# A gated linear-attention block and an MLP on one core: v's scratch copied in whole runs, two level masks in one multiply, and a new written-out order

## The chip, the core and the metric

The kernel runs on one core of a Trainium2 chip. The core has five engines that each run their own instruction stream in order and meet through semaphores: TensorE (PE, matrix products), VectorE (DVE, elementwise work on two operands), ScalarE (ACT, elementwise functions and copies), GpSimd (POOL) and SyncE (SP, which here issues every DMA). The metric is the device time of one execution in microseconds (us), taken as the median of repeated runs.

## What is computed

Inputs are float32: `q, k, v, a_re, a_im` of shape (4 batches, 8 heads, 768 tokens, 48), and an MLP with `w_in` (384 x 2048), `w_out` (2048 x 384) and `alpha` (2048).

```python
mag = np.sqrt(a_re * a_re + a_im * a_im)
scale = np.minimum(mag, 0.999) / (mag + 1e-06)
a_re_n, a_im_n = (a_re * scale, a_im * scale)
for t in range(S):
    ar, ai = (a_re_n[:, :, t, :, None], a_im_n[:, :, t, :, None])
    new_re = ar * S_re - ai * S_im
    new_im = ar * S_im + ai * S_re
    kv = np.einsum('bhd,bhe->bhde', k[:, :, t], v[:, :, t])
    S_re, S_im = (new_re + kv, new_im)
    y[:, :, t] = np.einsum('bhd,bhde->bhe', q[:, :, t], S_re)
x = y.transpose(0, 2, 1, 3).reshape(B * S, H * D)
h = x @ w_in
g = np.maximum(h, 0.0) + alpha * np.minimum(h, 0.0)
return g @ w_out
```

## The kernel before, in words

**Tiling.** The 768 tokens of a batch are cut into six chunks of 128, so there are 24 *units* u0 to u23 (batch 0 is u0 to u5, batch 1 is u6 to u11, and so on). A unit is one chunk of all eight heads. Units of a batch follow each other, because the state `St` goes from one to the next.

**Gates.** `gates` turns `a_re, a_im` into decays and rotations. It is called nine times: for batch 0 in pieces of one, two and three chunks, for each later batch in two pieces of three chunks. It writes decays to a DRAM scratch (`decs`, line 323) and rotations to another (`phs`, lines 421 and 431). The last VectorE instruction of a gate piece is the second L429; then `phs` is stored, and the first unit of that piece loads it as `PP` (L587) before it can begin with its L661. u0, u1, u3, u6, u9, u12, u15, u18 and u21 are the units that stand first behind a gate piece.

**A unit.** It loads `KQ` (keys and queries, L579 and L581), `PP` (L587), `T` (decays, L594), `V` (L603 to L608) and `VL` (L626 and L629). VectorE rotates keys and queries (L661, L663). Then three *visits* handle two levels each: (1, 2), (4, 8) and (16, 32). At level h the queries in the second half of each block of 2h tokens meet the keys of its first half: copies into `WQ` or `W` on ScalarE (L740, L756), 16 small matmuls per level into `ps_lv` (L678), and a decay step of all keys and queries on VectorE (L717, six per unit). What does not belong to the block is cleared by a mask: levels 1, 2, 4, 8 by a VectorE multiply that reads `ps_lv` and writes the tile `A` (L702, one per level), levels 16 and 32 by ScalarE copies with per-row scales (L699). Then transposes of the keys (L785, with copies L787 and L788), the state update (L797, L826, L829), and the output `ps_y` from the masked scores (L808 opens it, L817 multiplies `A` by `VL` over the six levels) and from the state (L841). ScalarE copies `ps_y` into the unit's `T` tile (L855), which is stored to the DRAM scratch `ysc` (L860).

**VL and its scratch.** `VL` holds, for each level, the rows of v that are keys there. Levels 1, 2 and 32 are loaded from v (ten DMAs, L626). Levels 4, 8 and 16 (`SPREAD`) come from a DRAM scratch `vsc`, which `half_rows` fills from v: for each batch, level and pair of heads one DMA (L560) picks the rows of all six chunks, in pieces of 96 floats. For chunk 0 of batch 0 there is a smaller scratch of its own, filled first by 12 DMAs. A unit reads its part of the scratch with one DMA into 128 partitions (L629).

**MLP.** Units are grouped: m0 is u0, m1 is u1, m2 is u2 and u3, and so on in pairs up to m11, then m12 is u22 and m13 is u23. Once the units of a group have stored `ysc`, it is loaded as `xT` (L873). For each of 16 blocks of 128 features, `features` does three matmuls (L889), a ScalarE step (L896) and a VectorE step (L898), and `outputs` multiplies by `w_out` into `ps_o` (L908). `ps_h` has two buffers, so TensorE can be two blocks ahead of L898. The weights arrive as 64-bit words and are rebuilt as float32 by ScalarE, GpSimd and VectorE (L507 to L519) during the first 180 us.

**The order.** All this is written as generators (tasks). Each `yield` marks a step. `ORDER` is one string in which a letter stands for a task (A to I the gate pieces, J the loads of units, K `half_rows`, L `loads_v`, M the raw weights, N and O the two weights' rebuilding, P to Z and a to m the units, n the loads of `xT`, o the MLP). `plan.run(ORDER)` advances the named task by one step per letter, and so sets the order of instructions on every engine and of the DMAs on SP's queue. The arguments of `DVE(...)`, `ACT(...)`, `DMA(...)`, and the rings `R[...]`, were inputs for making the string; when the kernel is built they do nothing. Semaphore waits are put in afterwards from the tiles that instructions share.

Of the kernel before, what the change touches and what calls it, by code (L numbers as in the profile page):

```python
# [18 lines left out]
P = 128  # L19
# [11 lines left out]
    "AAAAAAAAAMJBMMMMMAAAAAAAAAOAAAAAKAAAABAAAAAAAAAKAAKAKKKKKKKKKAAOAKBOKOBOBJAANBNAABBBNAAAOAAAAAANNAMA"  # L31
    "AAAAKNANABNNAAAANBAAAAABJBBBANABMBMABAOAONJOABAAABBBBBMBAAAABAAOBAABAABBBBKOBBBBBBBBBNNNNNBBJNBBPBBN"
    "BOBBBJJOJOOONBBBBPPBPBLBBLLOBPCCBBBBBLLKLLNNNJPPPCBBBBBBLPBBBBBPBPBBLLLLMPOCBMCBBPPPBBMBBCCCCLBKBBLN"
    "KNKOBKBBCBCPCCCBBCCCCCCOOCOPCCKCCJOCCPCPDDCCJJCPPCOPCPPCDNNNNDMJPJPPCPPPPPPPPPPPPPCNCQCPJOOCQOCMDDDD"
    "DCLOPCPLPPLLCQLKQJLCQLCMCQJDKLLLJQQJCQNQPCPPPPPQQQCDDCQQCNONCNKQCQQMCOOLOOCOQQJCDDDDQCnOKOOJOCRLOOCo"
    "ooQLQQCCCRDLQQQQKQQDKCDMoCNDCQKQQQDDQQQQCRCOCoLRooRooCLOLCDDLCLLDLCLLoLCDDDDCRRCoLJoJJQoCCRooCCLoKLJ"
    "ooooCoooCLRRooCooCRCQCRQQQQQQCDRQQRoooooRRCCRCCCoooCoRRoCCRQRCRNNNNRRCRRRRRRRRRRRRRNMNCNNRNNCDRDoooo"
    "oRooJDNNooooDRooRORDRoOOooODOSooooJJooEoSoRRRoooSoDooooOooEoSSSSSSoooooJNLLLLJLLLELSDSoEDEEooooSooSR"
    "SSSooDEoooSSnSDooooooooRooJDJJSSSSSSSSSSSSJTLSLDEooLLDDDDLLDJTDSDDDDDDSSSSJSToSSSEoooooooSoTooTSSSDS"
    "JJSTJJEESSKTooLooooLoTTTLLooooooJTJoooUTTLTToToToToDTDDoDoDDKDoDKLLLLLLooooLoLoLnUEEoUoDooUooTTTTToo"  # L40
    "DEoDUTDooUooUoTTTTTooJoooEooooTTEoEEooooTTTTUTTUUUUooDTDEDDoDDoDDDDLDLDoDoooDLoKUUKToLELELoTTTUUoooE"
    "LoLooLLDLUDooooLDoUDEEDEEEoEoEooooUooDDDDoDooUUKUUUooooooLJTUUUUoooUDTTTTUToooJDJooDDDDoDoooUUooEUUU"
    "UUUFoEooEUooEoooEooooJoEJEFoEEoEoooUUooEEEoUooUUUUUoEooEoEEVooooooooooooEoVVFEoVJooJJJJJooooFFJnoVFo"
    "oooJoVVVoJJVJLoooLLLVLooLLVVVLooLoFLEEEEEEEVEEEEEEEELEEEWEWEEJoEooEooooVVVFFVooooWooooVVooVWoooooooo"
    "VEWVEVoVoWWVVVFFVVFoEooWoooVLVoooLLFVooVVVVWWWVVVVJLLLWWWLLEEEWooLWWWWoLEoLLLoXoLoEEEEFEooooooVVWWWW"
    "WWVVWVoVXoWWVVoVoVoooooFLooLLJoJJFJEEFEEEWEEEoooEoEEoooWoWoKooooWWWWWWWWooWKWFWWXWWXoooWooFXXXXLoooX"
    "XXXooFFLLLLLLLLLWLWELELoooooooooFoFXEXooFooJWEoXFoXXonooooooFFLFJJJFXFoXoFooJJJoJJXXoXFXGooooooooXXo"
    "FFFooFXXXXXooFoFFooXFoooFooYXXXXXXXXXXXXXXXXXXoooFoYYYGFJJooFLoooYYYFFFFFFYYooooLLYooGooYooooZJJJYKJ"
    "GZooYGJYYYYooFLFFFFFLFLLLFLooooFZoYYoooooooZZZZZYYYYoYYLYLLZZoooGJZLLYoYooFYoFYFoooFYYoFZGKoFoFFFKFo"
    "oZZZYKKKZYYYYYYYGLGZZoFFKKZKoKFFFFFFFoFFFLLLLLoLLFoFoooZZoZZYYYYLooZooooFGoooLYFFGYYYZYoFFFFFFoooGLL"  # L50
    "ooooooLaLZZZnoFJoZoJoooJFFFFFZZFZooooooooGoooooGZGZZZZZZZZZZZZZLZZaoaoGZoGooLGoooooooooooaaaaaJoJoLJ"
    "ooJJGoGoaJaabbJJJoobooooLoooLaoaaaaaooGoooooaabbLLLLLLGLGoooooHHoooooaaaaaaLoGoGGGGGaaaoGGoGaooaooob"
    "oGHoGaaobGbbabobbaaaaaoooaooLLLLbooGoGbbHHbGaGaGaaGoaoaoaaoobbbbLooGoGGGGJGJJGGGoGJJGoGJGoGJoGHooooo"
    "oboooooooooHHHLLLLcccnooooHocoobbbbbbbccbHcoooJbooJHoooLLocLbbLoLoGoooocbcobcKooooooHHdHbbbbKbGLbGGG"
    "GbGGbGGLGGGGLbbbLGbbbbbbLLoGoHHHHoHooLLLLoooKccccccooocoHLooooocoooccocHLGGGdoGGoooHJJHGHGHGGHGLdcoc"
    "coccHcccHLHooooHoooocoddddccccccdoHLLcHcLLLLLLGGLLoLooooLLdGdLGGdGGGoGooKoooddcdccccccccHcGdGdoodooo"
    "oHoooooooooGGGGooooooooHoooodoooonKooodoooodddddddGooooHJooJHHoddddoJJJJJJJoooJIoodooeddddddddHddedd"
    "ddddddeooooooooJeJJJLJJJoooooeoeeooeooooooHeeHeHeHHHHHHHoooooooooooLooeLeeeLLLHeoLHfHHoHHLofoooooooo"
    "oooeoLeofLoJooLoLooeLfeLffeeeeeoeoeHoHoHHKHHHHHHHHHHJeooeeoofefeeeeeffHIHIHeHeHeHeeeeeeeeeoJogfoofJL"
    "LoLoooLfLffffLoLooLooLLffLooKoKKoooooooHHHHHoofffogHoHIHHfoLoLfHLIofoKgIoooooHoogggggHoofffffgogHHoH"  # L60
    "HnHogHoooooooffoofffffofgggJfLLLLLoooogggggofofoooogHHgJLLIIfoffLLLoooHooHfgffLooJffooIoLHooLoIggoII"
    "oIooooggoooooIIIIooooogooogoogoogogIIIgooogggggggIggoJIJJJhgJhgogoogKIIhhhhoJoIooogIohIIhhhgILLLhhoo"
    "ohJLJJJJLLLLLoooLLLoooooooLoKoooioohiohhhoohhooihhooooIoooohhhIiIIiiohoooooiIioIhiIoooooLhhhhhhJJIJJ"
    "ooiiooonhhoooooohhhhhohLhhhhhhLLLhhIhIihhoLJLoJJJJLIIIIIIIIIIIIIIIIIooiiiiioooooooojIoooooooooiooooL"
    "LiooojojLjLooIIIIIIIILIIIIIIILoooojijioioioojjLiiiiiojooiioooooooIoIioIIoiojjjoooooiiiiiiiiiiiIIIIII"
    "LILiiiLLooLLLLoooLIIIIIIIIILoojjLooojjiiiLLoooooooIojjoLIIjoooooooIooIIJJJonooojjjjjjjjJjJooooooJooo"
    "oooojooojjooooojjjjjjjLjjjjjjjjjjjkokooooookoooooookkkkooLoooooookookokokooLLLLJLLookJooLLLLoookkooo"
    "ooJJJJJJkokkkooooookoooookkkkkkkkkooooookokooooookoLoLkkkkkkkLLlkJkkkkkkkkkkLLooloooLLLooLoLoJoooJoo"
    "ooooooooollllolloooolloJoJoolloooooooooolllllmloooLnooooLooooooLoooLllllooollllmloooooooolooollooooo"
    "ooooolloooooLmomllllllllllllllllLloLLLLLLoooLmmLmLmoooLoooommoomoooooooomoonoooooooooLoooooooooommmm"  # L70
    "mooLoooooooooooooommoooommmoommoomoomooooooooooommmmoooooooommoooooooommmmmmmmmmmmmmoooooooooooooooo"
    "oooooomoooooooooooooooooooooooooooooooooooooooooooonoooooooooooooooooooooooooooooooooooooooooooooooo"
    "oooooooooooooooooooooooooooooooooooooooooooooooooooooooooooooooooooooooooooooooooooooooooooo")
# [28 lines left out]
def kernel(  # L102
# [64 lines left out]
    masks, by_row = {}, {}  # L167
# [3 lines left out]
    def mask(h):  # L171

        m = work.tile([P, P // h, h], F32, tag="WQ0", name="mask", bufs=1)
        nc.gpsimd.memset(m, 1.0)
        nc.gpsimd.affine_select(out=m, in_=m, pattern=[[-h, P // h], [0, h]], base=0,
                                channel_multiplier=1, compare_op=ALU.is_ge, fill=0.0)
        nc.gpsimd.affine_select(out=m, in_=m, pattern=[[h, P // h], [0, h]], base=h - 1,
                                channel_multiplier=-1, compare_op=ALU.is_ge, fill=0.0)
        masks[h] = consts.tile([P, HC], F32, tag=f"mask{h}", name=f"mask{h}")
        flat = m.rearrange("p n h -> p (n h)")  # L180
        for i in range(2):
            nc.gpsimd.tensor_copy(masks[h][64 * i:64 * i + 64],
                                  flat[64 * i:64 * i + 64, HC * i:HC * (i + 1)])
# [22 lines left out]
    for name in LEVELS:  # L206
        R[name] = Ring(2 if name <= 4 else 1)
# [286 lines left out]
    def to_f32(dst, *key):  # L494
# [25 lines left out]
        slots.append(slot)  # L520
        return t
# [19 lines left out]
    def half_rows():  # L541


        for b, chunks in [(0, 1)] + [(b, NCH) for b in range(B)]:
            vsc = dram.tile([len(SPREAD), chunks, 2, HC, 2 * D2], F32, tag=f"vsc{chunks}", name="vsc")
            for c in range(1 if (b, chunks) == (0, NCH) else 0, chunks):
                vsc_of[b * NCH + c] = vsc[:, c]
            for i, h in enumerate(SPREAD):
                for n in range(HP):
                    src = v[b, n].rearrange("(m s h) c e -> s m h c e", s=2, h=h)[0]  # L550
                    src = bass.AP(tensor=src.tensor, offset=src.offset + NCH * D2, ap=src.ap)
                    dst = vsc[i, :, n // 2, :, (n % 2) * D2:(n % 2 + 1) * D2].rearrange(
                        "c (m h) e -> m h c e", m=src.shape[0])
                    if chunks == 1:
                        dst, src = dst[:, :, 0], src[:, :, 0]

                    k = (HP * i + n) * NCH // (HP * len(SPREAD))
                    end = yield DMA(24.5 * chunks, ("KQ", (b - 1) * NCH + k) if b else
                                    ("raw", "in", k // 3 if chunks == 1 else k))
                    nc.sync.dma_start(dst, src)  # L560
            for c in range(1 if (b, chunks) == (0, NCH) else 0, chunks):
# [35 lines left out]
    def loads_v():  # L597
        for u in range(NU):
# [13 lines left out]
            for k, h in enumerate(LEVELS):  # L612
                for i in range(2):
# [8 lines left out]
                    for dst, src in runs:  # L622
                        if not first:
# [3 lines left out]
            t = yield DMA(98 * len(SPREAD), ("halves", u))  # L627
            k = LEVELS.index(SPREAD[0])
            nc.sync.dma_start(VL[:, k:k + len(SPREAD)].rearrange("p l n e -> p l (n e)"),  # L629
                              vsc_of.pop(u).rearrange("l i t e -> (i t) l e"))  # L630
# [14 lines left out]
    def unit(u):  # L645
# [37 lines left out]
        def mask_out(name, t, e):  # L683

            n = HC

            if name in by_row:
                e = yield ACT(HP * name + 100, e, takes=(R[name],))
            else:
# [311 lines left out]
```

## Time and profile before

| what | value |
|---|---|
| median of 3 runs | 852.85 us (852.84 to 853.85) |
| span of the profiled execution | 853.8 us |
| PE busy | 702.5 us (82%), 11,488 records |
| DVE busy | 650.8 us (76%), 1,020 instructions |
| ACT busy | 441.3 us (52%), 937 instructions |
| POOL busy | 203.3 us (24%) |
| DMA | 130.91 MB, 153 GB/s on average |
| DMA packets | 194,174, of them 74,120 under 512 B |

"Busy" is the time in which at least one instruction of the engine was running. A float32 matmul leaves two records, one per pass, so 1,344 records of L889 are 672 matmuls. The span is the profiled execution's own time; it lies 0.1% above the median of the runs. In the profile the letter after an engine's name, as in SPq, stands for its instruction queue.

### The profile page before, as it was taken

Reading aid. Unit: us, or ns where it says so; the run is one execution under the profiler, and the core shown is the slowest. Engines: PE = TensorE matmul, PEld = TensorE weight load, DVE = VectorE, ACT = ScalarE, POOL = GpSimd, SP = SyncE. Lnnn points to the kernel's source line nnn. Section 1 sums busy time; section 2 is a strip of 40 time slices with the busy share of each in tenths; the row PEclk is TensorE's granted clock in tenths of the full one; section 3 lists DMA queues with packets and bytes.
Section 4 is the critical chain, followed back from the end, with each engine's and each line's share of the span. In section 5 each row is a group of like instructions: output and inputs, shape, how many; then the busy total and the mean of one; then the engine's idle time right before and its main releaser. Section 6 shows DMA issues by size and latency. Waiting matters only on the chain.

```text
span 853.8 us, 26837 instructions
## 1 busy us (share of the span) xinstructions
PE 702.5 (82%) x11488; PEld 534.1 (63%) x11488; DVE 650.8 (76%) x1020; ACT 441.3 (52%) x937; POOL 203.3 (24%) x293
## 2 busy tenths in 40 slices
PE   0000428678999898999999799999999999999998
PEld 0000416557777676776677577777777777777776
DVE  5999989998998799778999686788896754643212
ACT  7848786565736444564567333456544333332211
POOL 6322142306526202440036400530006100000000
PEclk9999858689999999899999899999999999999999
DMA  6796784875398369747874479357654455421000
GB/s 202 235 245 211 219 226 137 246 188 142 98 275 182 77 159 242 187 112 182 222 202 105 129 195 206 96 144 192 151 174 100 135 132 133 108 51 35 20 28 10
DMA packets 194174, 130.91 MB, mean 153 GB/s; under 512 B 74120, under 2 KB 185864, under 8 KB 194056
## 3 DMA queue, kind: packets, MB, share of 16 engines
q1 hardware_dynamic: 194056, 129.20, 57.8%
q8 instruction: 90, 1.47, 0.7%
q14 instruction: 28, 0.23, 0.1%
HBM read 100.82 MB, written 35.71 MB: 160 GB/s over the span
## 4 chain that ended last, share of the span: by engine, by line
PE 62%; DVE 17%; DMA 11%; issue 4%; ACT 3%; SPq 2%; DVEq 0%; ACTq 0%
PE ps_o L908 24%; PE ps_h L889 23%; DVE KQ L717 4%; PE ps_lv L678 4%; PE ps_y L817 4%; DMA T<-decs 4%; PE ps_kv L797 3%; PE ps_y L841 2%; DVE gate L426 2%; PE ps_kt L785 2%; DMA PP<-phs 2%; DMA gate<-in_a_re_dram 1%; DVE gate L298 1%; DMA phs<-gate 1%; DVE gate L318 1%
## 5 line engine op out<-in xcount | busy, mean ns | idle before, releaser
L889 PE MATMUL ps_h<-xT,w_in_sb 128*128 128x256 f32 (+1 forms) x1344 | 305.3, 358 | 10.7 <-DMA xT<-ysc 8.2
L908 PE MATMUL ps_o<-w_out_sb,g_sb 128*128 128x384 f32 x768 | 293.8, 498 | 5.2 <-DVE g_sb L898 4.2
L889 PEld LDWEIGHTS ps_h<-xT,w_in_sb 128*128 128x128 f32 x1344 | 234.6, 194 | 82.9 <-DMA xT<-ysc 8.4
L898 DVE SCALAR_TENSOR_TENSOR g_sb<-g_sb,al,ps_h 128x256 f32<-128x256 f32 (+1 forms) x224 | 97.2, 436 | 116.9 <-ACT g_sb L896 116.5
L896 ACT ACTIVATE g_sb<-ps_h 128x256 f32<-128x256 f32 (+1 forms) x224 | 78.7, 352 | 204.3 <-PE ps_h L889 203.1
L717 DVE TENSOR_TENSOR KQ<-KQ,T 96x1024 f32<-96x1024 f32 x120 | 148.1, 1234 | 40.3 <-PE ps_lv L678 34.5
L908 PEld LDWEIGHTS ps_o<-w_out_sb,g_sb 128*128 128x128 f32 x768 | 139.4, 193 | 58.7 <-DVE g_sb L898 7.9
L678 PE MATMUL ps_lv<-WQ 96*32 96x32 f32 x2304 | 34.0, 202 | 78.7 <-DVE WQ L661 50.6
L678 PEld LDWEIGHTS ps_lv<-WQ 96*32 96x32 f32 x2304 | 26.1, 115 | 99.2 <-DVE WQ L661 50.6
L740 ACT COPY WQ<-KQ 96x1024 f32<-96x1024 f32 x48 | 50.0, 1042 | 27.0 <-DVE KQ L717 26.8
L515 POOL TENSOR_SCALAR top<-top 128x768 f32<-128x768 f32 x16 | 45.8, 2862 | 73.5 <-ACT top L507 62.8
L855 ACT COPY T<-ps_y 48x256 f32<-48x256 f32 x96 | 30.9, 364 | 51.6 <-PE ps_y L841 50.9
L817 PE MATMUL ps_y<-A,VL 64*48 64x64 f32 x2304 | 45.4, 232 | 14.4 <-issue 13.4
L338 POOL TENSOR_TENSOR gate<-gate 128x72 f32<-128x72 f32 x42 | 27.5, 654 | 118.1 <-ACT gate L368 115.3
L817 PEld LDWEIGHTS ps_y<-A,VL 64*48 64x48 f32 x2304 | 43.1, 133 | 15.4 <-issue 14.2
L338 DVE TENSOR_TENSOR gate<-gate 128x576 f32<-128x576 f32 (+5 forms) x84 | 47.9, 571 | 1.3
L699 ACT ACTIVATE A<-ps_lv,columns 128x64 f32<-128x64 f32 x144 | 36.9, 335 | 20.4 <-PE ps_lv L678 20.4
L756 ACT COPY W<-KQ 96x512 f32<-96x512 f32 x48 | 30.7, 639 | 30.0 <-DVE KQ L717 24.9
L426 DVE TENSOR_TENSOR gate<-gate 128x1152 f32<-128x1152 f32 (+2 forms) x36 | 43.4, 1231 | 2.1 <-POOL gate L411 2.0
L678 PE MATMUL ps_lv<-KQ,W 96*32 96x32 f32 x1536 | 24.3, 204 | 17.8 <-ACT W L756 15.8
L702 DVE TENSOR_TENSOR A<-ps_lv,mask 128x256 f32<-128x256 f32 x96 | 37.4, 411 | 0.0
L787 ACT COPY T<-ps_kt 128x384 f32<-128x384 f32 x48 | 23.1, 480 | 26.8 <-PE ps_kt L785 26.7
(106 smaller groups left out, 904.8 us busy)
## 6 DMA issues: line engine op xcount, KB each, us to landing
T<-decs SPq DMA_DIRECT2D x48, 384.0 KB
PP<-phs SPq DMA_DIRECT2D x24, 387.0 KB
KQ<-in_q_dram SPq DMA_DIRECT2D x48, 192.0 KB
decs<-gate SPq DMA_DIRECT2D x7, 1152.0 KB
phs<-gate SPq DMA_DIRECT2D x14, 576.0 KB
KQ<-in_k_dram SPq DMA_DIRECT2D x40, 192.0 KB
vsc<-in_v_dram SPq DMA_DIRECT2D x48, 144.0 KB
VL<-vsc SPq DMA_DIRECT2D x24, 288.0 KB
```

Of the source, the lines that this page charges most:

```text
L338: on(4 * k).tensor_tensor(out=m, in0=w[:, 1::-1].unsqueeze(2).to_broadcast([P, 2, 2, k]), in1=pairs_of(u), op=ALU.mult)
L426: TT(out=m[:, a], in0=U5[:, 1 + a], in1=turned(off3, o)[:, a].unsqueeze(1).unsqueeze(3).to_broadcast([P, L // 2, nb, 2]), op=ALU.mult)
L515: nc.gpsimd.tensor_scalar(out=top, in0=top, scalar1=F64_SMALL, scalar2=None, op0=ALU.max)
L678: nc.tensor.matmul(t[64 * i + j:64 * i + j + HC // 2, p], lhsT=keys(n, g), rhs=queries(n, g), start=True, stop=True)
L702: nc.vector.tensor_tensor(out=a.rearrange("p n (g t) -> p n g t", g=2), in0=t.unsqueeze(2).to_broadcast(whole), in1=masks[name].rearrange( ...
L717: nc.vector.tensor_tensor(out=x, in0=x if x0 is None else x0, in1=m, op=ALU.mult)
L740: nc.scalar.copy(z.rearrange("p i n t -> p i (n t)").rearrange("p i (m h) -> p m i h", h=h), bass.AP(tensor=KQ.tensor, offset=KQ.offset + ...
L817: nc.tensor.matmul(o, lhsT=Vp[h][64 * i:64 * i + 64, s, e_ * D:(e_ + 1) * D], rhs=a, start=False, stop=False)
L889: nc.tensor.matmul(p, lhsT=w_in_sb[:, f // 2, kk, f % 2 * P:(f % 2 + 1) * P], rhs=x_of[m][:, kk], start=(kk == 0), stop=(kk == NK - 1))
L896: nc.scalar.activation(gt, p, AF.Relu, scale=-1.0)
L898: nc.vector.scalar_tensor_tensor(out=gt, in0=gt, scalar=al_1[:, f:f + 1], in1=p, op0=ALU.mult, op1=ALU.add)
L908: nc.tensor.matmul(sums[0], lhsT=gt[:, c * P:(c + 1) * P], rhs=w_out_sb[:, f], start=(f == 0), stop=(f == NF - 1))
```

## The change

Three things are changed, and `ORDER` is replaced.

1. `half_rows` copies per batch, level and *two* pairs of heads one run of rows: source and destination have h whole rows of v (all six chunks, h x 2,304 bytes in one piece). There are 24 such DMAs, 288 KB each, where there were 60 (48 of 144 KB and 12 of 24 KB). The scratch has a new layout with the pair of heads outermost and the chunk inside, and the separate scratch for the first chunk is gone. A unit now reads the scratch in two DMAs, one for each half of the partitions, in pieces of 96 floats where they were 192.
2. The two masks of a visit lie in one tile, and one VectorE multiply clears both levels. Levels 1 and 2 share an `A` tile with two buffers, levels 4 and 8 one with a single buffer (level 4 had two, level 8 one).
3. `ORDER` is a new string of 4,232 letters; the old one had 4,292. Nearly every letter stands elsewhere. The rings' counts follow.

```diff
 ORDER = (
-    "AAAAAAAAAMJBMMMMMAAAAAAAAAOAAAAAKAAAABAAAAAAAAAKAAKAKKKKKKKKKAAOAKBOKOBOBJAANBNAABBBNAAAOAAAAAANNAMA"
...
+    "AAAAAAAAAAAAAJJMABBBAAAAAMMMMJJMLABBAAAAAAAABAABAAAANBBAAAAAAABABBNBNOBNABNANAABBBOANOOBABBBBBMABABAO"
...
-        masks[h] = consts.tile([P, HC], F32, tag=f"mask{h}", name=f"mask{h}")
+        at, first = VISIT[h]
+        if h == first:
+            pairs[first] = consts.tile([P, 2, HC], F32, tag=f"mask{h}", name=f"mask{h}")
+        masks[h] = pairs[first][:, at]
...
-        for b, chunks in [(0, 1)] + [(b, NCH) for b in range(B)]:
-            vsc = dram.tile([len(SPREAD), chunks, 2, HC, 2 * D2], F32, tag=f"vsc{chunks}", name="vsc")
-            for c in range(1 if (b, chunks) == (0, NCH) else 0, chunks):
-                vsc_of[b * NCH + c] = vsc[:, c]
+        one = NCH * D2
+        for b in range(B):
+            vsc = dram.tile([HP // 2, len(SPREAD), 2, HC, NCH, D2], F32, tag="vsc", name="vsc")
+            for c in range(NCH):
+                vsc_of[b * NCH + c] = vsc[:, :, :, :, c]
             for i, h in enumerate(SPREAD):
-                for n in range(HP):
-                    src = v[b, n].rearrange("(m s h) c e -> s m h c e", s=2, h=h)[0]
...
-                    nc.sync.dma_start(dst, src)
+                for s in range(HP // 2):
+                    rows = v[b, 2 * s]
+                    src = bass.AP(tensor=rows.tensor, offset=rows.offset + one, ap=[[2 * h * one, P // h], [1, h * one]])
+                    end = yield DMA(150)
+                    nc.sync.dma_start(vsc[s, i].rearrange("n (m h) c e -> (n m) (h c e)", h=h), src)
...
-            t = yield DMA(98 * len(SPREAD), ("halves", u))
             k = LEVELS.index(SPREAD[0])
-            nc.sync.dma_start(VL[:, k:k + len(SPREAD)].rearrange("p l n e -> p l (n e)"),
-                              vsc_of.pop(u).rearrange("l i t e -> (i t) l e"))
+            for i in range(2):
+                t = yield DMA(49 * len(SPREAD), ("halves", u))
+                nc.sync.dma_start(VL[HC * i:HC * (i + 1), k:k + len(SPREAD)].rearrange("p l n e -> p (l n) e"),
+                                  vsc_of[u][i].rearrange("l n t e -> t (l n) e"))
...
+        def mask_both(visit, t, e):
+
+            first = visit[0]
+            e = yield DVE(2 * HP * HC, e, takes=(R[first],))
+            a = work.tile([P, 2, HP, HC], F32, tag=f"A{first}", name=f"A{first}", bufs=2 if first == 1 else 1)
+            whole = [P, 2, HP, 2, HC // 2]
+            nc.vector.tensor_tensor(out=a.rearrange("p l n (g t) -> p l n g t", g=2), in0=t.unsqueeze(3).to_broadcast(whole),
+                                    in1=pairs[first].rearrange("p l (g t) -> p l g t", g=2).unsqueeze(2).to_broadcast(whole),
+                                    op=ALU.mult)
+            for at, h in enumerate(visit):
+                A[h] = a[:, at]
             made.append(e)
             return e
...
-            for h, ta, e in tiles:
-                e = yield from mask_out(h, ta, e)
+            if visit[0] in pairs:
+                e = yield from mask_both(visit, shared[0], e)
+            else:
+                for h, ta, e in tiles:
+                    e = yield from mask_out(h, ta, e)
```

Line numbers in the changed kernel are four or five higher than before from the middle on; the text keeps the numbers of the kernel before.

## The prediction

> **What bounds the kernel now.** I read the engine totals first, then the 40 slices, then the windows of 50 us, and at last the waits of single lines.
>
> ```profile
> span 853.8 us, 26837 instructions
> PE   0000428678999898999999799999999999999998
> DVE  5999989998998799778999686788896754643212
> PEclk9999858689999999899999899999999999999999
> ...
> PE 62%; DVE 17%; DMA 11%; issue 4%; ACT 3%; SPq 2%; DVEq 0%; ACTq 0%
> ```
>
> TensorE does nothing for four slices, fills up by the ninth and stays full to the end; VectorE is full from the second slice to about the twelfth. Two stages, then: first VectorE sets the pace, later TensorE does. The windows (length, then busy time and count of PE, PEld, DVE, ACT, POOL, then granted clock, DMA share, GB/s) put numbers on it.
>
> ```profile
> 50.00:100.00 50.00, 9.73 (x346) 8.22 (x346) 49.00 (x87) 39.60 (x55) 13.42 (x8) 1.00 0.81 232
> 100.00:150.00 50.00, 25.71 (x656) 21.55 (x656) 45.68 (x89) 37.20 (x64) 15.34 (x8) 0.66 0.65 180
> 150.00:200.00 50.00, 38.40 (x798) 30.71 (x799) 46.58 (x67) 28.73 (x61) 13.71 (x18) 0.80 0.74 205
> 200.00:250.00 50.00, 47.73 (x865) 37.41 (x865) 47.51 (x72) 28.89 (x72) 21.96 (x29) 1.00 0.59 165
> 250.00:300.00 50.00, 44.68 (x720) 33.51 (x719) 38.76 (x53) 29.36 (x63) 21.20 (x34) 0.97 0.65 142
> 500.00:550.00 50.00, 50.00 (x870) 38.02 (x869) 37.96 (x55) 20.15 (x51) 13.31 (x32) 1.00 0.75 184
> ```
>
> Of 151.3 us without PE work (853.8 - 702.5), 90.3 lie before 100 us, 24.3 and 11.6 in the next two windows.
>
> I turn this into one figure per unit. TensorE's work has the same instructions in both kernels. At full clock the chain shows 1.29 us for six records of L889 at 256 columns (0.43 per matmul; I take 0.22 at 128) and for four of L908 (0.645 per matmul), some 1.3 for 96 of L678, 1.4 for 96 of L817, 1.9 for 64 of L797, 0.94 for 32 of L841. Over the whole program that makes 692.2 us. The moment when a unit opens its output (its first L808) plus the PE work that still stands behind it in the order is a floor for the end. In the trace of before this floor rises so: u0 96.9 + 686.6 = 783.5; u1 132.9 + 677.6 = 810.5; u2 823.1; u3 832.4; u4 836.1; u5 836.1; u6 837.7; u7 842.0; u8 840.9; u12 847.0; u14 853.5, and about 850 from there on. Most is lost by u4, under VectorE's pace; a new order can earn by putting more PE work in front of these moments, or by letting VectorE reach them sooner.
>
> **Part 1, the double mask.** The rows:
>
> ```profile
> L702 DVE TENSOR_TENSOR A<-ps_lv,mask 128x256 f32<-128x256 f32 x96 | 37.4, 411 | 0.0
> L829 DVE TENSOR_TENSOR St<-St,ps_kv 96x384 f32<-96x384 f32 x44 | 24.1, 547 | 11.1 <-PE ps_kv L797 8.6
> L898 DVE SCALAR_TENSOR_TENSOR g_sb<-g_sb,al,ps_h 128x256 f32<-128x256 f32 x160 | 75.4, 474 | 69.0 <-ACT g_sb L896 68.7
> L661 DVE TENSOR_TENSOR WQ<-KQ,PP 96x1024 f32<-96x1024 f32 x24 | 29.4, 1227 | 4.9 <-DMA PP<-phs 4.9
> ```
>
> No row has 512 elements out of PSUM. 256 cost 411 ns and 384 cost 547, 1.06 ns per element, which leads to 683 at 512. Bounds: half of L661's 1,227, or 614, with no fixed cost at all; and 822, with nothing saved. I take 683, being a short extrapolation from two rows of the same operation. 48 x (822 - 683) = 6.7 us less VectorE work in all (0 to 10.0), 0.28 per unit, so 1.4 by u4. It is inside the VectorE sums below.
>
> [...]
>
> Level 4's second `A` buffer goes. The multiply for u+1 then waits for u's L817, as level 8's already did; L717 of level 16 and any L898 queue behind it on VectorE. u's L817 stand well ahead of it in the new order, so I price it at 0; without that cover it is one L717 step, 1.2 us, per unit.
>
> **Part 2, the scratch.**
>
> ```profile
> L560 SPq DMA_DIRECT2D vsc<-in_v_dram x60: 562/643/1972, 6.5 to 617.7; - x60
> L629 SPq DMA_DIRECT2D VL<-vsc x24: 383/428/746, 70.2 to 772.4; - x24
> ```
>
> (Counts, then minimum, median and maximum ns of the issue.) SP's queue loses 36 x 0.643 = 23.1 us and gains 24 x 0.428 = 10.3. The trace's packets of 384 B take 26.2 ns on average, of 768 B 44.6, of 3,072 B 138. Sixty copies were 19,200 packets of 384 B, 31.4 us of all 16 DMA engines; now 7.08 MB in long runs, at the 3,072 B rate 19.8. Runs over 3,072 B of tensor data are not in the trace; if they bring nothing it stays at 31.4. The unit's loads become 18,432 packets of 384 B instead of 9,216 of 768 B: 30.2 instead of 25.7. Net 7 us less of some 490 (4 more at the worst). None of it stands on the chain once units run; on the end it is 0, hidden behind TensorE (its only wait on `VL<-vsc` is 1.0 us), and up to 1 us either way without that cover. Only u0 could feel it: its `VL` now needs all six copies of the batch. SP's row for that load is 67 in both orders, with 75 us of 16-engine DMA time issued up to it where there were 57; at the 0.81 of the 50 to 100 window that is 93, plus some 3 to land, while u0 opens its output at about 101 (below). 0 to 3 us, taken as 0.
>
> **Part 3, the order.** VectorE's work up to a unit's last L717 is summed over the two orders with the rows' durations (times 0.936: in before 695.7 us of durations make 650.8 busy). The floor that follows, if VectorE's idle time stayed as in before:
>
> | unit | VectorE moves by | PE work left, before, after | floor, before, after |
> |---|---|---|---|
> | u1 | +1.4 | 677.6, 669.5 | 810.5, 803.8 |
> | u2 | -5.3 | 662.3, 651.7 | 823.1, 807.2 |
> | u4 | +4.4 | 616.5, 599.5 | 836.1, 823.5 |
> | u6 | -2.9 | 554.1, 548.5 | 837.7, 829.1 |
> | u8 | -8.2 | 503.1, 504.4 | 840.9, 834.0 |
>
> The new order has 8 to 17 us more MLP work in front of u1 to u5. It doesn't get all that, because it also moves waits:
>
> ```profile
> DVE WQ L661 <- DMA PP<-phs: 4.9, 4, 2.0
> ...
> PE ps_h L889 <- DMA xT<-ysc: 8.2, 1, 8.2
> ```
>
> (Waited in all, times, longest.) (a) From the end of a gate piece's last L429 to the first L661 behind it, before takes 9.2 us at u0, 10.0 at u3 and u15, 10.3 at u21, 12.5 at u6, where the chain shows why:
>
> ```profile
> 241.78 3.33 DMA phs<-gate
> ...
> 245.59 8.51 DMA PP<-phs
> ```
>
> Two DMAs stand between, so some 9 us is the least. Before has 8.7 us of VectorE work in that gap at u0, after 6.0: 3.2 us more wait, and all units' VectorE work queues behind. u0 opens its output near 96.9 + 2.6 + 3.2 = 102.7 if nothing absorbs it, 101 if the idle time in before around there does. (b) At u1, TensorE's levels 16 and 32 stand behind the first three blocks of m0, which wait for `xT`; I work out its arrival at 120 (u0's output 107, ScalarE's L855 behind two gate steps to 113, two DMAs), and L717 waits for those levels: another 2 us, some taken back by the denser MLP. I take 3.5 us for (a) and (b) together from u1 on, 0 to 7 as bounds: the floor at u8 becomes 837.5, 3.4 under before. (c) At u6 the gap has 7.5 us of VectorE work where it had 11.6; TensorE's run-ahead covers it.
>
> From u8 to the end before loses 853.8 - 840.9 = 12.9 us. I let after lose the same, minus nothing and plus (d): at u12 the gap holds 1.9 us of work and two L898 where it held 14.7 and five. At TensorE's pace (two blocks with their outputs, 2 x 2.6 us) 5.2 of the 9 pass, VectorE waits 4 (to 7) at L661, L898 queues behind, and TensorE, two `ps_h` buffers ahead, would lose stall + 2.4 (L661, L663) + 0.5 - 5.2, so 1.7 (0 to 4.7). Before had its own stall there (a 6.9 us `St` load on the chain), so I take 0.5.
>
> Sum: 837.5 + 12.9 + 0.5 = 850.9 against the profiled 853.8, -2.9; from the median 852.85 that is **850.0 us**. What a measurement of this kernel can tell from no change is 0.2%, or 1.7 us, so 850.0 lies just on the faster side.
>
> **The rivals.**
> *The early work pays in full* (b and a absorbed, since TensorE, busy without a break from 120 us on, holds its full clock where before was granted 0.66 and 0.80). The floor at u8 stays 834, the end 846.9, or 846 from the median. For it: the table. Against: the gap of u0, which no other work fills.
> *What is won early is lost by u8.* TensorE saturates later anyway (before's floor rises only 5 from u4 to u8); if a + b cost 7, the end is 853.5.
> *Slower: gate pieces arrive too late.* One mechanism, at the L661 of u6, u12 and u21: the new order leaves 7.5, 1.9 and 3.0 us of work in gaps that had 11.6, 14.7 and 5.0. With 12.5 us from L429 to L661, as at u6 before, VectorE waits 5, 7.3 and 5; TensorE loses the wait minus 2.3 each time, 2.7 + 5 + 2.7 = 10.4, and with (a) at its upper bound, 3.5 more: 850 + 14 = 864. It decides once the wait at L661 exceeds the 2.3 us that two blocks cover. Half of it gives 857. For it: the DMA queues are busy 0.6 to 0.8 of the time, and such short gaps leave no room for a late `PP`. Against: in before such waits are only 4.9 us over all.
> *It doesn't do what it says:* long runs are cut up and the double mask costs 822. VectorE has 6.7 us more than above, 2.2 by u8: 852.
>
> **How the numbers follow.** Sum as above, 850: 0.28. Early work in full, 846 and better: 0.20. Lost by u8 or no gain from parts 1 and 2, 852 to 855: 0.17. Gates too late, 856 to 864: 0.35, as three gaps are exposed and each only needs one late load. Faster than 851.1: most of the first two, 0.45. Within 0.2%: 0.13. Slower than 854.6: 0.42. The range runs from 840 (the nominal floor at u8 with a third of the later loss saved) to 863; the likeliest case's own is 846 to 854.
>
> **What would show it.** PE busy in 100 to 150 over 28 and in 150 to 200 over 42; u0's first L808 at 99 to 104, u8's floor at 834 to 841; `xT` of m0 near 120. L702 at 683 ns, 48 of them. `DVE WQ L661 <- DMA PP<-phs` at 10 to 20 us with its longest at u12, and PE idle under 3 us there; 10 us of PE idle near the gaps means the slower rival. The sum is wrong if u1's or u2's first L808 comes more than 7 us after 133 and 161, or if TensorE loses over 17 us behind u8.

## The result and the profile after

| | before | changed |
|---|---|---|
| median | 852.85 us (844.81 to 853.85) | 911.06 us (905.39 to 915.6) |
| ratio, 95% interval | 1 | 1.067 (1.060 to 1.075) |
| profiled span | 853.8 us | 908.8 us |
| TensorE busy, idle | 702.5, 151.3 us | 725.3, 183.5 us |
| time waited for DMAs by PE and DVE, all lines | 23.0 us | 83.2 us |

Medians here and below are over all runs, while ratios and intervals leave out the few that ran in a slower state. The change is slower by 6.7%, far outside the forecast of 850 and its range. The page of the changed kernel, with the lines that answer to those of before (span, the slices of PE, DVE and the granted clock, and the chain that ended last):

```profile
span 908.8 us, 26777 instructions
PE   0001468878979897999889779999888989999998
DVE  6989989787976895999678769788556754543212
PEclk9999879799989998999999789999998999999999
...
PE 33%; DMA 24%; DVE 23%; SPq 9%; ACT 5%; issue 5%; POOL 1%; DVEq 0%; ACTq 0%
```

TensorE starts a little earlier, but has 7s and 8s through the middle of the run where it had 9s. The chain, which ran over TensorE for 62% of the span, now does so for 33%; DMA and SP's queue hold 33% where they held 13%. The windows of 50 us (length, PE, PEld, DVE, ACT, POOL busy, granted clock, DMA share, GB/s):

```profile
100.00:150.00 50.00, 34.89 (x843) 28.70 (x839) 45.26 (x92) 32.55 (x62) 7.16 (x3) 0.80 0.53 140
150.00:200.00 50.00, 37.90 (x664) 28.80 (x664) 43.23 (x64) 29.84 (x63) 6.30 (x14) 0.90 0.75 212
250.00:300.00 50.00, 40.67 (x704) 30.04 (x704) 34.79 (x49) 16.85 (x40) 14.82 (x30) 0.93 0.81 198
500.00:550.00 50.00, 39.74 (x388) 28.27 (x389) 35.21 (x46) 22.06 (x39) 2.27 (x6) 0.83 0.56 157
```

The early work is there (34.9 us of PE in 100 to 150, 25.7 before). What is new is 500 to 550: 39.7 us where TensorE was busy for all 50, at a granted clock of 0.83 and in a window in which VectorE has three tenths of its time free. The waits name DMAs (us in all, times, longest):

```profile
DVE KQ L719 <- DMA T<-decs: 23.0, 10, 4.8
DVE WQ L661 <- DMA PP<-phs: 18.1, 8, 5.1
PE ps_h L894 <- DMA xT<-ysc: 17.0, 6, 4.9
PE ps_y L822 <- DMA VL<-vsc: 10.3, 9, 2.3
DVE St L727 <- DMA St<-in_v_dram: 7.1, 3, 5.2
```

Before had 5.0, 4.9, 8.2, 1.0 and 1.4 in these places. How one such wait costs more than itself is best seen once, in the timeline (start, duration, engine, line; in brackets the idle time before it and what ended it):

```profile
495.29 0.56 SPq L435 DMA_DIRECT2D phs<-gate  x1
495.89 0.58 SPq L592 DMA_DIRECT2D T<-decs  x1
...
498.80 0.70 PE L894 MATMUL ps_h<-xT,w_in_sb 128*128 128x256 f32 x2
503.52 1.22 DVE L719 TENSOR_TENSOR KQ<-WQ,T 96x1024 f32<-96x1024 f32 x1 [4.85 <-DMA T<-decs]
504.67 0.54 DVE L834 TENSOR_TENSOR St<-St,ps_kv 96x384 f32<-96x384 f32 x1
505.26 1.09 PE L846 MATMUL ps_y<-KQ,St 96*48 96x64 f32 x16 [5.77 <-DVE St L834]
```

u14's second T load is issued at 495.89, behind a gate store, and lands 7.5 us later. u14's L719 waits for it 4.85 us; *u13's* state update L834 needs nothing from that load but stands behind L719 on VectorE; TensorE needs L834 and is idle for 5.77. The two windows behind it show the rest of the bill:

```profile
499.50:505.30 5.80, 0.04 (x2) 0.04 (x2) 1.74 (x3) 0.52 (x1) 0.00 (x0) 0.69 0.67 169
505.30:512.10 6.80, 6.80 (x90) 5.00 (x91) 6.38 (x7) 1.67 (x6) 0.00 (x0) 0.52 0.08 29
```

For the 6.8 us after the gap the granted clock is 0.52: four records of L913 (L908 before) take 2.93 us in it, at 507.30, and 1.45 behind it, at 512.25. I estimate another 3.3 us lost (6.8 x 0.48). Between 230 and 830 us the trace's clock record has 11 such spells at 0.5, 55 us, where before had 3, 17 us: up to 19 us of work time (half of the 38 more). It adds up: from 250 us to the end, TensorE is idle for 59 us where it was for 23, and busy for 19 us longer; 36 + 19 is the whole 55 between the two profiled executions. The length of a gap alone does not tell what follows: one of 1.8 us at 598.6 had 3.4 us at a granted clock of 0.51 behind it, and one of 2.1 us at 453.1 had 3.4 us at 1.00. (The last section has where these two lie.)

The prediction's floor (first L808 of a unit, L813 in the changed kernel, plus the PE work behind it) puts the loss in place. The forecast column is the prediction's table plus its 3.5 us for the waits (a) and (b); the last is the old order with both code parts, run below.

| unit | before | after, forecast | after | old order, new code |
|---|---|---|---|---|
| u1 | 810.5 | 807.3 | 806.4 | 808.6 |
| u2 | 823.1 | 810.7 | 813.8 | 822.0 |
| u4 | 836.1 | 827.0 | 833.0 | 833.3 |
| u5 | 836.1 | – | 834.7 | 833.3 |
| u6 | 837.7 | 832.6 | 843.5 | 834.7 |
| u8 | 840.9 | 837.5 | 855.4 | 840.2 |
| u12 | 847.0 | – | 865.6 | 841.3 |
| u14 | 853.5 | – | 880.8 | 840.6 |
| u19 | 851.4 | – | 897.8 | 839.7 |
| span | 853.8 | 850.9 | 908.8 | 842.6 |

Up to u5 the new order is a little ahead of before. From there it loses 74 us to the end (908.8 - 834.7), where before loses 18.

### The profile page after: what moved, and what is told of

The parts are those of the page before. It is cut to its first block, busy times and chain, and to the rows that moved or that the text cites. A ratio compares the mean times of both kernels' runs of the same rounds, so it can differ in the third digit from the quotient of the medians.

```text
span 908.8 us, 26777 instructions
## 1 busy us (share of the span) xinstructions
PE 725.3 (80%) x11488; PEld 541.4 (60%) x11488; DVE 648.5 (71%) x972; ACT 437.5 (48%) x937; POOL 206.3 (23%) x293
## 4 chain that ended last, share of the span: by engine, by line
PE 33%; DMA 24%; DVE 23%; SPq 9%; ACT 5%; issue 5%; POOL 1%; DVEq 0%; ACTq 0%
PE ps_o L913 13%; PE ps_h L894 13%; DMA T<-decs 8%; DVE KQ L719 5%; DMA ysc<-T 4%; SPq L624 3%; DMA VL<-vsc 3%; DVE gate L430 2%; DMA xT<-ysc 2%; DVE gate L342 2%; PE ps_y L822 2%; PE ps_lv L678 2%; PE ps_y L846 2%; DVE g_sb L903 2%; DMA phs<-gate 1%
## 5 line engine op out<-in xcount | busy, mean ns | idle before, releaser
L894 PE MATMUL ps_h<-xT,w_in_sb 128*128 128x256 f32 (+1 forms) x1344 | 311.5, 365 | 19.6 <-DMA xT<-ysc 17.0
L913 PE MATMUL ps_o<-w_out_sb,g_sb 128*128 128x384 f32 x768 | 305.1, 512 | 10.3 <-DVE g_sb L903 9.6
L894 PEld LDWEIGHTS ps_h<-xT,w_in_sb 128*128 128x128 f32 x1344 | 240.2, 198 | 99.0 <-DMA xT<-ysc 12.8
L913 PEld LDWEIGHTS ps_o<-w_out_sb,g_sb 128*128 128x128 f32 x768 | 141.5, 197 | 66.5 <-DVE g_sb L903 13.2
L719 DVE TENSOR_TENSOR KQ<-KQ,T 96x1024 f32<-96x1024 f32 x120 | 148.5, 1239 | 35.0 <-PE ps_lv L678 23.4
L822 PE MATMUL ps_y<-A,VL 64*48 64x64 f32 x2304 | 47.3, 229 | 24.9 <-issue 14.6
L519 POOL TENSOR_SCALAR top<-top 128x768 f32<-128x768 f32 x16 | 43.1, 2697 | 100.2 <-ACT top L511 57.9
L822 PEld LDWEIGHTS ps_y<-A,VL 64*48 64x48 f32 x2304 | 42.4, 129 | 27.7 <-issue 15.9
L661 DVE TENSOR_TENSOR WQ<-KQ,PP 96x1024 f32<-96x1024 f32 x24 | 30.1, 1253 | 28.8 <-DMA PP<-phs 18.1
L860 ACT COPY T<-ps_y 48x256 f32<-48x256 f32 x96 | 32.1, 365 | 38.2 <-PE ps_y L846 37.4
L719 DVE TENSOR_TENSOR KQ<-WQ,T 96x1024 f32<-96x1024 f32 x24 | 30.0, 1252 | 23.7 <-DMA T<-decs 23.0
```

Source lines behind the costliest of these rows:

```text
L519: nc.gpsimd.tensor_scalar(out=top, in0=top, scalar1=F64_SMALL, scalar2=None, op0=ALU.max)
L719: nc.vector.tensor_tensor(out=x, in0=x if x0 is None else x0, in1=m, op=ALU.mult)
L822: nc.tensor.matmul(o, lhsT=Vp[h][64 * i:64 * i + 64, s, e_ * D:(e_ + 1) * D], rhs=a, start=False, stop=False)
L894: nc.tensor.matmul(p, lhsT=w_in_sb[:, f // 2, kk, f % 2 * P:(f % 2 + 1) * P], rhs=x_of[m][:, kk], start=(kk == 0), stop=(kk == NK - 1))
L913: nc.tensor.matmul(sums[0], lhsT=gt[:, c * P:(c + 1) * P], rhs=w_out_sb[:, f], start=(f == 0), stop=(f == NF - 1))
```

## Experiments

**1. Order against code.** The order's letters count steps, so an order fits other code if that code has the same steps. For the old order, the new code got bare steps where it has fewer, and both `VL` loads in the step of the one; for the new order, the old code got two masks or two copies in one step. PE, ACT and POOL then have the same instructions in the same order as in the kernel whose order it is. In the new order the old scratch is the one for whole batches alone, without the separate one for the first chunk.

```diff
-                    end = yield DMA(150)
+                    end = yield DMA(150)
+                    yield
...
-            for i in range(2):
-                t = yield DMA(49 * len(SPREAD), ("halves", u))
+            t = yield DMA(98 * len(SPREAD), ("halves", u))
+            for i in range(2):
                 nc.sync.dma_start(VL[HC * i:HC * (i + 1), k:k + len(SPREAD)].rearrange("p l n e -> p (l n) e"),
```

New order, old masks, old scratch: 

> The new order with the kernel before's masks (one multiply per level, both in the step of the double one, level 4 with its second buffer) and the old scratch (48 copies of 144 KB, two per step; VL by one load; no separate scratch for the first chunk). Theory O, the order alone makes the loss, because loads are placed where they land just as they are needed: 895 to 915 us, PE busy in 500 to 550 us under 45. Theory S, the long copies and the two-part load of VL make it: under 875 us. Theory M, the shared A tiles make it: under 875 us here too, and the next two kernels tell S from M.

New order, double mask, old scratch: 

> The new order and the double mask, but the old scratch copies and the one-part load of VL. Theory O: 895 to 915 us, within 8 us of the changed kernel. Theory S: under 875 us. Theory M: 900 us or more.

Old order, both parts new: 

> The old order with the double mask and the new scratch (one copy of 288 KB in every second step of the old ones, both loads of VL in the step of the one). Theory O: 843 to 858 us, the prediction's own value of both parts being -3 to +2 us. Theory S or M: over 870 us.

Old order, scratch new: 

> The old order and the old masks with the new scratch alone. Theory O: 846 to 860 us. Theory S: over 870 us. Theory M: within 5 us of the kernel before, as S has no part in it. VL's first load then waits for six copies of 288 KB instead of twelve of 24 KB: if that is late, PE's first work on u0's output moves behind 100 us.

Old order, mask new: 

> The old order and the old scratch with the double mask alone. The prediction's part 1 took 6.7 us from VectorE's work, 1.4 of it by u4: 848 to 852 us by that and L702 at 683 ns. If the lost second buffer of level 4 or the late first mask costs more than this, over 853 us.

Old order, both parts again: 

> Both parts of the change in the old order again, with more rounds, for the interval: the same instructions as in the run of that kind before, 841 to 848 us, faster than the kernel before by 0.5 to 1.3%. Scratch alone had 846.6, so the mask should add 0 to 4 us to it.

| order | masks | scratch | median, us | ratio to before, 95% |
|---|---|---|---|---|
| old | new | old | 854.1 | 1.001 (0.999 to 1.004) |
| old | old | new | 846.6 | 0.996 (0.993 to 1.000) |
| old | new | new | 844.7; again 844.0 | 0.989 (0.983 to 0.995); 0.992 (0.989 to 0.995) |
| new | old | old | 937.0 | 1.098 (1.092 to 1.104) |
| new | new | old | 934.4 | 1.093 (1.085 to 1.100) |
| new | new | new | 911.1 | 1.067 (1.060 to 1.075) |

The order alone makes the loss: +67 us with the new code, +85 with the old. Theories S and M are out: the new order with both old parts takes 937.0 us where they asked for under 875, and the old order with both new parts 844.7 where they asked for over 870. Theory O had the direction and missed the size, as the new order with the old scratch came out 23 to 26 us above the changed kernel and outside the 895 to 915 that I gave. The double mask alone in the old order gave 854.1, over the 848 to 852 expected, but the kernel before had 852.8 beside it: no gain and no loss that can be told. The old order with the new code is faster than both kernels, than the one before by some 1%. Its page (span, slices of PE, chain):

```profile
span 842.6 us, 26778 instructions
...
PE   0000438679999899999999999999999999999998
...
PE 69%; DVE 16%; DMA 6%; issue 4%; ACT 3%; SPq 1%; DVEq 0%; ACTq 0%
```

TensorE is full from the tenth slice on but for one 8 and the last, and PE and DVE wait for DMAs about 15 us in all.

**2. Where in the order.** All steps depend on each other alike in both orders, so one order's beginning can be followed by what is left in the other's sequence. The cut is u5's last step.

```diff
-ORDER = NEW
+ORDER = NEW[:1234] + (the steps left, in OLD's sequence)
```

Then the reverse, with the first 1,221 steps of the old one. 

> The changed kernel's code; its order up to the last step of u5, and from there every remaining step in the old order's sequence. Theory A, the new order loses behind u5, all along the run, because there each unit's loads are used as soon as they can land: 838 to 850 us, as the new order's first part is no worse than the old one's (floor at u5 834.7 against 836.3). Theory B, the first part leaves something behind (loads queued late on SP, work begun too early) that the rest pays for: over 870 us.

> The reverse: the old order's sequence to the last step of u5, then the new order's. Theory A: 895 to 915 us, the whole loss back, with waits of PE and DVE for DMAs of 70 us or more. Theory B: under 865 us.

New then old: 862.2 us (1.019, 1.009 to 1.029). Old then new: 898.3 (1.063, 1.052 to 1.074), with 66 us of DMA waits on PE and DVE. The second is as theory A has it, the waits a little under its 70. The first is between the two expectations, and the floor tells why: it has 838.7 at u5, 859.7 at u6, and 861.7 at u23. The seam costs 21 us at one place, where L661's 6.6 us for u6's `PP` is the longest wait for a DMA, and the old order behind it loses nothing more. So the second part of the new order is what loses, all along.

**3. T's round trip.** T has two buffers; u's output is copied into its T tile (L860) and stored from there, and only then can T be loaded for u+2.

```diff
-                    yT = T[:, 0:4, 0:P].rearrange("p (i s) t -> p i s t", i=2)
+                    yT = T[:, 0:4, 0:P] if u < 6 else tops[1][:, 0:4 * P].rearrange("p (a t) -> p a t", a=4)
+                    y_out, yT = yT, yT.rearrange("p (i s) t -> p i s t", i=2)
...
-                              T[64 * e_:64 * e_ + D, 0:4, 0:P])
+                              y_out[64 * e_:64 * e_ + D])
```

> The changed kernel, but from u6 on the output goes from ps_y to a tile that the weights no longer need, and is stored from there, so that T is free for the unit after the next when the state update has read it. The order is the same, so T's loads stand where they stood on SP's queue, behind the store. Theory T, the round trip from one unit's output through its T buffer to the T of the unit after the next is what loses most: no large change yet, 895 to 911 us, since SP still issues the load behind the store. Rival, other loads (PP, VL, xT) lose as much: 900 to 915 us.

The second kernel also has T's loads further ahead in the order. 

> The same, with T's two loads moved forward on SP's queue from u8 on, to just behind the last read of the buffer by the unit before the last (by up to 74 letters of the order). Theory T: 870 to 890 us, DVE's waits for T under 8 us instead of 23. Rival: DVE's waits for T fall as much, but the time only goes to 898 to 912 us, as the next load is late then, and the waits for PP, V, VL and xT stay or grow.

Measured 901.5 us (1.065, 1.056 to 1.074), which fits theory T and its rival alike, and 887.0 (1.047, 1.040 to 1.055) with the loads ahead, as theory T has it. The waits of the second:

```profile
DVE WQ L661 <- DMA PP<-phs: 19.7, 8, 5.3
PE ps_h L895 <- DMA xT<-ysc: 19.3, 6, 4.5
...
DVE KQ L719 <- DMA T<-decs: 2.4, 4, 0.8
```

The wait for T went from 23.0 to 2.4 us and the time by 24.1, so this wait was paid about in full; 9.6 of the 24.1 us had come with the tile alone, when the wait for T was still 20 us. The waits for `PP` and `xT` grew by some 2 us each. T's round trip is a third of the 67 us, where theory T had it as what loses most.

**4. A dose of lateness.** One more copy, which nothing reads, in front of each unit's T loads, in both orders.

```diff
+                    late = dram.tile([D, H, TL], F32, tag="late", name="late")
+                    nc.sync.dma_start(late, scr.rearrange("(h d) c s -> d h c s", d=D)[:, :, at])
```

> The old order with the changed kernel's code, and one more DMA on SP's queue in front of each unit's two loads of T: a copy of 384 KB from the decay scratch to a scratch that nothing reads, 24 in all, which makes T later by its issue (0.6 us) and its share of the queue (2 to 3 us by its size at 150 to 200 GB/s); it is set against the same copies in the new order. Theory A, the old order holds slack behind its loads and the new one none: here the 24 x 2.6 to 3.6 us = 62 to 86 us of lateness cost less than a quarter, so 845 to 863 us. Rival, every order of these units passes lateness on as the new one does: 880 us or more.

> The same copies in the changed kernel, with its own order. Theory A: half or more of the 62 to 86 us is passed on, 940 to 990 us. Rival: as much as in the old order, within 10 us of the difference there.

Old order 859.2 us, 15.2 more than without (844.0); new order 932.5, 21.5 more. The wait for T rose from 1.3 to 5.7 us in the old order and from 23.0 to 35.5 in the new. By the ratios to before the dose costs 1.4% (1.006 against 0.992) and 2.6% (1.094 against 1.067). The waits go theory A's way, and so does the old order's time, but the new order's is under the 940 that I gave, and the two costs differ by 6 us (11 by the ratios), about the 10 that the rival allowed: theory A is not borne out here. The dose was smaller than I took it for, and the old order paid for it too, half of it (8.1 us of floor) between u12 and u15. No wait for T shows there; TensorE stops for 5.3 us amid u14's L817, in a wait like the one of experiment 6. How much more slack the old order has is not shown by this.

**5. Without the loads.** From u8 on, `PP`, `T`, `V` and `VL` are not loaded; the tiles of u6 and u7 are used again.

```diff
-            L["PP"] = PP = work.tile([D2, H, P + 1], F32, tag="PP", name="PP", bufs=1)
-            nc.sync.dma_start(PP, phs.rearrange("(h d) i s -> (d i) h s", d=D)[:, :, at * P:(at + 1) * P + 1])
+            L["PP"] = PP = old["PP"] if u >= 8 else work.tile([D2, H, P + 1], F32, tag="PP", name="PP", bufs=1)
+            old["PP"] = PP
+            if u < 8:
+                nc.sync.dma_start(PP, phs.rearrange("(h d) i s -> (d i) h s", d=D)[:, :, at * P:(at + 1) * P + 1])
...
```

> The new order with the output in a tile of its own (901.5 us when run alone), but from u8 on the loads of PP, T, V and VL are left out; the units compute with what u6 and u7 loaded, so this leaves out those loads and the right values, and no step of PE, DVE, ACT or POOL. Theory L, late loads make the loss: behind u8 only the xT round trips are left, so it ends near u8's floor of 855 us plus some 8, 855 to 872 us. Theory E, the steps of the engines themselves wait for each other in the new order: 880 us or more.

> The same left out in the old order with the same code (844 us with all loads). Theory L: 838 to 845 us, as its loads land in time anyway. Theory E says the same here; a fall to under 835 would mean that the old order pays for its loads too.

> The new order, output in its own tile, from u8 on only V's and VL's loads left out (14 or 15 of a unit's 21 or 22 DMAs, so SP's queue is mostly free). Theory L with SP's queue as what makes loads late: 865 to 880 us, the waits for T and PP falling too. Theory L with the transfers and the buffers as what makes them late: 888 to 900 us, the waits for T and PP staying at 35 us.

> The new order, output in its own tile, from u8 on only PP's and T's loads left out (3 DMAs of 387 and 384 KB each per unit, 1.15 MB of its 2.1). Theory L with the transfers and buffers: 868 to 885 us. With SP's queue: 885 to 898 us.

| left out from u8 on | new order | old order |
|---|---|---|
| nothing | 901.5 | 844.0 (output in T) |
| V, VL | 872.3 | |
| PP, T | 860.3 | |
| all four | 852.3 | 834.1 |

With no loads to wait for, the new order loses 49 us less, and the slices of PE are full from the sixteenth on but for the last:

```profile
PE   0000358578897989999999999999999999999998
```

Its floor is 848.5 at u8 and 844.6 at u23: behind u8 nothing is lost. That is theory L, with 3 us more gain than it asked for; every step of the engines stands where it stood. The two parts bring 29 and 41 us, more together than both at once. With V and VL gone the waits for T behind 230 us fall from 19.4 to 2.2 us although T is loaded as before, but those for `PP` only from 12.1 to 10.7; with `PP` and T gone the time falls further than either version of theory L gave. So the 14 or 15 small DMAs of V and VL do help to make T late, and the loads cannot be priced one by one. The old order gives 9.9 us too, and comes under the 835 that I had named as the sign that it pays for its loads as well. Leaving them out pays in both orders, but five times as much in the new one.

**6. The same cure for the faster kernel.** The old order with the new code, output in its own tile, and T's loads ahead for seven units. 

> The old order with the changed kernel's code, the output in its own tile from u6 on and T's loads moved forward where they can be (seven units, by 3 to 98 letters). In the old order DVE waits for T 1.6 us in all, so by theory L nothing is to be had there: 841 to 847 us, the same as without. If it comes under 839 us, T's round trip costs the old order too, through SP's queue and not through a wait for T itself.

850.5 us (0.997, 0.993 to 1.001; without it 0.992, 0.989 to 0.995): no gain, over the 841 to 847 expected, and by the medians 6 us *slower* than without, though the intervals touch. The floor jumps by 6.5 between u14 and u15, where TensorE waits 5.0 us at an L822 (L817 before), and the trace puts this down to no semaphore. Before has a stop of 4.0 us of this kind, at u13's L817, and its trace does show what comes just before the end of it: a 16 KB packet of the DMA queue for instructions is through at 483.61 us, and TensorE goes on at 484.99. The DMA engines were busy for 0.57 of the 7 us before. That TensorE waited for its own code is my guess; no run tried this, nor why the packet came when it did.

## Why the prediction was wrong, step by step

- **The failing step** is "From u8 to the end before loses 853.8 - 840.9 = 12.9 us. I let after lose the same". After loses 53.4 there (908.8 - 855.4), far over the 17 that the prediction named as the sign of a wrong sum. The 12.9 is a property neither of the units' work nor of the old order: from u8 to the end the new code loses 2.4 us in the old order (842.6 - 840.2), and 0.5 us in the new one once the loads are left out (849.0 - 848.5). About half of the 12.9 (6 us of floor between u13 and u14) lies at one stop of TensorE in u13's L817, of the kind of experiment 6, with 6.1 us at a granted clock of 0.50 behind it:

```profile
484.99 0.66 PE L817 MATMUL ps_y<-A,VL 64*48 64x64 f32 x11 [4.00 <-issue]
```

  I carried the loss of one order over to another without asking what time the new one leaves each load.
- The same step fails from u5 to u8 already: 4.8 us in before, 20.7 in after, with `PP` at u6, V at u8 and `xT` of m4 as the waits (5.1, 5.3 and 4.3 us). Here the table held VectorE's idle time at that of before, and the first two of these waits are new idle time of VectorE.
- **The early part was right up to u1.** u0's first L808 came at 100.5 (forecast 99 to 104), m0's `xT` was issued at 118.6 and used at 121.1 (120), u1's floor is 806.4 (807.3), and PE busy in 100 to 150 is 34.9 (over 28). In 150 to 200 it is 37.9, under the 42 that I asked for, and by u4 the floor is 6 us above the forecast; the gain over the old order with the same code is gone by then (833.0 against 833.3).
- **The slower rival** had the right kind of event and the wrong number of places. It looked only at `PP` behind gate pieces. There L661 waits 5.1 us at u6, 2.0 at u12 and 1.8 at u21; in all 18.1, inside the announced 10 to 20, but longest at u6 and not at u12. I had taken 14 us as the most that this could cost (its 5 us for u21 don't follow from the 3.0 us of work given there: 12.5 - 3.0 is 9.5); T, `xT`, `VL`, V and `St` are late as well, together 65 of the 83 us.
- **Cover.** The prediction let two MLP blocks (5.2 us) cover a wait on VectorE. In the timeline above a wait of 4.85 us at L719 left TensorE idle for 5.77, because the instruction that TensorE needed next was queued behind L719; and the granted clock of 0.52 in the 6.8 us after it is in no term of my sum.
- **Part 1, the double mask,** is sized right as an instruction:

```profile
L702 DVE TENSOR_TENSOR A<-ps_lv,mask 128x512 f32<-128x512 f32 x48 | 32.6, 679 | 0.0
```

  679 ns where I worked out 683. Alone in the old order it changes the time by nothing that can be told (0.999 to 1.004).
- **Part 2, the scratch,** was priced at 0 on the end, up to 1 us either way without cover. Alone in the old order it is worth up to 0.7%, with the mask 0.5 to 1.1%, and in the new order 23 us (934.4 to 911.1). The copies were not cut up: they are 448 packets of 9,216 to 36,864 bytes and take 22.4 us of the 16 DMA engines (19.8 worked out). That the saved SP time and DMA traffic count as soon as loads are late fits this, but which of them does was not tried; I had seen TensorE as a cover that would hold.
- **What can be told from no change** was put at 1.7 us. The four runs of before in the table above lie 9 us apart, so a change of the forecast's size would hardly have been told from nothing by a few runs.

What the short leads come from is shown only in part. From the issue of a unit's second T load to its first L719 there are 9.0 us in before (median; 5.8 to 22.8) and 6.7 in after (4.5 to 11.3), while T's pieces on the changed kernel's chain take 3.7 to 8.1 us, but for one of 1.7: a lead that fits the middle of that spread leaves a wait in ten of the 24 units. That the order was worked out for median durations fits this, but no run changed the durations that it was worked out for. Without loads the new order is still 18 us behind the old one, half of it lost before u8, where the loads are still there; the rest stays open.

## What to carry to other kernels

A written-out order fixes, for each load, the time between the moment its buffer comes free and its first use; compare those leads with the spread of the load's landing times, for every load in both orders, before summing anything else. In VectorE's order here a late load stopped work that doesn't need it (4.85 us at u14's L719 held up u13's L834, and TensorE for 5.77), so the loss of one order says nothing about another. Judge a new order and new code apart: here the code is worth -0.8% and the order +8%.

## What was not expected of the hardware

In the changed kernel a granted clock of 0.5 follows gaps that look harmless: 1.8 us idle at 598.6 had 3.4 us at 0.51 behind it, and one wait of 5.8 us cost 6.8 us at 0.52 on top. Another of 2.1 us, at 453.1, had no such spell behind it. In the traces the two differ in where they fall. Between 230 and 830 us the clock records of before and of the changed kernel have 14 spells at 0.5: eight of 3.41 us, five of 6.83 and one of 10.24, and within a record they begin whole multiples of 3.41 us apart. With each trace cut into stretches of 3.41 us that begin where its spells do, TensorE was idle for 1.79 us or more in the stretch ahead of 13 spells and for 1.45 ahead of the other; stretches at full clock with no spell behind them had 1.66 us idle or less. The 1.8 us lie in one stretch, the 2.1 us are split over two, 0.7 and 1.3. No run moved a gap to try this, and single spells in other runs' traces don't fit.

Some waits of TensorE end just behind a packet of the instruction queue. In the traces of before and of the changed kernel it is idle for over 1 us without a semaphore 8 times behind 230 us, and each time it goes on 1.2 to 1.5 us after a 16 KB packet of that queue was through. No run tried whether the packet is the reason. In before these waits are 10.9 of the 23 us idle, in the changed kernel 6.7 of 59, so they are not what the new order loses.

And two sets of loads that bring 29 and 41 us when left out singly bring 49 together: T's lateness went away when V and VL weren't loaded.
